# A written order for three engines through the third chunk's heads, narrower expert widths, an early drain

## The chip, the cores and the metric

The kernel runs on one core of a Trainium2 chip. The metric is device time in microseconds (us) of one execution; lower is better. Engines: PE (TensorE), DVE (VectorE), ACT (ScalarE), POOL (GpSimd) and SP (SyncE, which only starts transfers). Each takes its instructions from its own queue, in order, and waits for the others at semaphores.

## The reference

Three layers stand behind one another, all in float32:

```python
scores = scale * np.matmul(q, k.transpose(0, 1, 3, 2))     # 4 batches, 8 heads, 576 positions, 64 wide
scores = np.where(mask, scores + bias[None], -1000000000.0) # mask: 0 <= i - j < 128
attn = np.exp(scores - scores.max(-1)) ; attn = attn / (attn.sum(-1) + 1e-9)
x = attn @ v                                                # as (2304 tokens, 512)
x = (sigmoid(x @ w_gate) * (x @ w_val)) @ w_out             # 512 -> 1536 -> 512
expert_idx = argmax(normalised x @ normalised expert_emb.T / tau)
for e in range(8):
    mask = expert_idx == e
    h = np.maximum(x[mask] @ w1[e], 0.0)                    # 512 -> 1024
    out[mask] = gate_w[mask, None] * (h @ w2[e])            # 1024 -> 512
```

## The kernel before

The 2304 tokens are 18 blocks of 128, in chunks of 2, 2, 2, 4, 4 and 4 blocks. A product in float32 is made of three matmuls: each operand is split into a high part, rounded to the matmul's format, and a low part, the rest; high x high, high x low and low x high are summed. So each operand costs a copy (the high part) and a subtraction (the low part) on ACT, DVE or POOL.

**Attention.** The first two chunks are done in pairs of heads (`fast_s`, `fast_n`, `fast_t`, `fast_b`): scores on PE, a reduction with the bias on DVE, exponentials on ACT, the scaling of the rows by one over their sum (`scale_rows`: "v" is DVE, "p" is POOL, by the table `NE`; its two entries are for the two chunks), a transpose on PE, a copy by ACT into `ttf`, and the product with v. From the third chunk on each head is a slot `i`: `load_qkv`, `split_qkv`, `load_v`, `split_v`, `emit_s`, `emit_soft`, `emit_norm`, `emit_t` (transposes, and the parts `ph` on ACT and `pl` on DVE), `emit_pv` (the product with v) and `emit_x` (the head's output).

**Work between the heads.** The weights w_gate and w_val come as 64-bit words. `feed_w(n)` takes n conversion steps: `conv_b` (three DVE operations), and for every second step the split of a weight tile (`split_hi` on ACT writes `wh`, `split_lo` on DVE writes `wl`). `run_group` is one tile of the gated layer: `group_mm` (24 matmuls) and `group_post`. `GR` says how many groups follow each head, `FS` and `FW` how many conversion steps.

**What sets the order.** Inside `manual_schedule` the order of PE, DVE and ACT is that in which the code is written: this holds for the head pairs. POOL's and SP's queues, and everything behind that block, are ordered by a scheduler. `tc.issue_after(ins)` keeps what is written under it behind the instruction `ins` (in the scheduler's order). Before, the third chunk's first loads and splits are held behind the last instruction of four engines in pair `SLOW` (`marks`) and behind the last load of the second chunk.

**Experts.** The tokens are sorted by expert with indirect transfers on POOL. Experts are taken in order of their size as far as `CAPS` knows it: `CAPS[e]` is the number of columns that the e-th has in `ffn1` (the tiles `h`) and of rows in `ffn2` (the tiles `z`, one for 128 tokens, then scaled to `y` and scattered by an indirect transfer to `out`). If an expert has more tokens than its capacity, a loop at the end does the rest. The program ends with a closing block (line 1203) in which each engine executes DRAIN instructions.

Of the kernel before, what the change touches and what calls it, by code (L numbers as in the profile page):

```python
# [1 line left out]

# [1 line left out]

# [21 lines left out]
E = 8  # L26
# [4 lines left out]
KD = DM // P  # L31
KF = FF // P
KE = FE // P
CAPS = [384, 384, 384, 352, 320, 320, 288, 256]
TCOL = NBLK
MAXOV = 16
BIG = 2.0 ** 42
# [6 lines left out]
NFAST = 2  # L44
NWARM = 12
FW = [[0, 0], [0, 1], [0, 1], [0, 1], [1, 1], [1, 1], [0, 1], [0, 1]]
FG = [0, 0, 0, 0, 0, 0, 1, 1]
FS = [3] + [2] * 7 + [0] * 24
FIRST = [0, 1] * 6
SLOW = 5  # L50
NE = ["vpvp", "vpvp"]
NR = "aapp"
GR = [3, 2, 3, 2, 3, 2, 3, 2, 2] + [2, 1, 1, 2, 1, 2, 1, 2] + [2] * 15
CHUNKS = [2, 2, 2, 4, 4, 4]
# [4 lines left out]
def attn_ffn_moe(ctx: ExitStack, tc: tile.TileContext, qd, kd, vd, wgv, w_out, emb, tau, w1, w2, cst, ids, out):  # L59
# [36 lines left out]
    def hi_copy(eng, o, i):  # L96
        if eng == "a":
            nc.scalar.copy(o, i)  # L98
        elif eng == "v":
            nc.vector.tensor_copy(o, i)  # L100
        else:
            nc.gpsimd.tensor_scalar(out=o, in0=i, scalar1=1.0, scalar2=0.0, op0=ALU.mult, op1=ALU.add)
# [67 lines left out]
    def split_qkv(i):  # L170
        c, h = slots[i]
        b0, nb = chunks[c]
        n = nb * P
        lo = 0 if b0 else 1
        q_t, k_t = raw.pop(i)[:2]
        qs = ap.tile([P, 512], F32R, tag="qs", name=f"qs{i}")
        k1 = ap.tile([P, 640], F32R, tag="k1", name=f"k1{i}")
        k2 = ap.tile([P, 640], F32R, tag="k2", name=f"k2{i}")
        hi_copy("p" if c == NFAST else QE, qs[:, :n], q_t[:, :n])
        lo_sub("p", qs[64:128, :n], q_t[64:128, :n], qs[64:128, :n])  # L180
        ks = slice(lo * P, n + P)
        hi_copy("p" if c == NFAST else KE_, k1[:, ks], k_t[:, ks])
        lo_sub("v", k2[:, ks], k_t[:, ks], k1[:, ks])
        bias = bias_of(h)
        bsp = {}
        for j in range(nb):
            kind = {4: 1, 13: 1, 5: 2, 14: 2}.get(b0 + j)
            if kind:
                t = row(f"bsp{i}_{j}")[:, 0:256]
                hi_copy("p", t, bias)  # L190
                nc.gpsimd.memset(t[64:128, 0:192] if kind == 1 else t[:, 0:64], -BIG)
                bsp[j] = t
        spl[i] = (qs, k1, k2, bias, bsp)
# [152 lines left out]
    def load_fast(c, lo, hi):  # L346
        b0 = chunks[c][0]
        ts = slice(b0 * P, b0 * P + 256)
        if lo == 0:
            for dst, nm in ((fq, "fq"), (fk, "fk")):  # L350
                dst[c] = slot([P, 4, 256], F32, f"{nm}{c}")
        for dst, src in ((fq, qd), (fk, kd)):
            pairs = src.rearrange("(g u) d t -> u d g t", u=2)
            for u in range(2):
                half = slice(u * D, u * D + D)
                nc.sync.dma_start(dst[c][half, lo:hi, :], pairs[u, half, lo:hi, ts])

    def load_fast_v(c):
        b0 = chunks[c][0]
        t = slot([P, H, 2, D], F32, f"fv{c}")  # L360
        fv[c] = t
        return nc.sync.dma_start(t, vd[:, :, b0:b0 + 2, :].rearrange("h p b d -> p h b d"))
# [63 lines left out]
    def fast_b(c, g):  # L426
        b0, nb = chunks[c]
        n = nb * P
        nm = f"f{c}_{g}"
        tts, fks = fst.pop((c, g))  # L430
        o = pt("m", f"o{nm}", 3)
        kbs = list(range(-1 if fks[0] == 0 else 0, nb))
        for z, kb in enumerate(kbs):
            q0, q1 = max(kb, 0), min(kb + 2, nb)
            c0 = (2 * kb + 1 + (q0 - kb)) * P
            for u in range(2):
                nc.tensor.matmul(o[u * D:u * D + D, q0 * P:q1 * P], fv[(b0 + kb) // 2][:, 2 * g + u, (b0 + kb) % 2, :],
                                 tts[u][:, c0:c0 + (q1 - q0) * P], start=(z == 0), stop=(z == len(kbs) - 1),
                                 skip_group_check=True)
        xh, xl = split_x_hi(c, 2 * g + 1, n, o)  # L440
        return lambda: lo_sub("v", xl, o[:, :n], xh)
# [20 lines left out]
    def split_hi(f):  # L462
        wh, wl = slot([P, 2, KD, P], F32R, f"wh{f}"), slot([P, 2, KD, P], F32R, f"wl{f}")
        hi_copy("a", wh, w_a[f])
        w_t[f] = (wh, wl)

    def split_lo(f):
        wh, wl = w_t[f]
        lo_sub("v", wl, w_a.pop(f), wh)
# [53 lines left out]

    NS = len(slots)
    NW = 2 * KF
    wnext = [0, 0]

    def feed_load(n):
        while wnext[0] < min(NW, n):
            load_w(wnext[0])  # L530
            wnext[0] += 1

    def feed_w(n):
        for _ in range(n):
            j = wnext[1]
            if j > NW:
                return
            feed_load(j + 8)
            if j == 0:
                conv_a(0)  # L540
            if j < NW:
                conv_b(j)
            if j % 2 == 0 and j:
                split_lo(j // 2 - 1)
            if j + 1 < NW:
                conv_a(j + 1)
            if j % 2 == 1:
                split_hi(j // 2)
            wnext[1] += 1

    def run_group(c, fs, gv):
        group_post(c, fs, gv, group_mm(c, fs, gv))
# [3 lines left out]
    load_fast(0, 1, 2)  # L556
    load_fast(0, 2, 4)
    load_fast_v(0)
    feed_load(3)
    load_fast(1, 0, 4)  # L560
    last_load = load_fast_v(1)
    warm = cp.tile([P, 512], BF16, tag="warm", name="warm")
    nc.vector.memset(warm, 0.0)
# [8 lines left out]
    with tc.manual_schedule(engines={ENG.PE, ENG.DVE, ENG.Activation}):  # L572
        for _ in range(NWARM):
            nc.tensor.matmul(wp, warm[:, 0:P], warm, start=True, stop=True)
        pairs = [(c, g) for c in range(NFAST) for g in range(H // 2)]
        fast_s(*pairs[0])
        fast_s(*pairs[1])
        fast_n(*pairs[0])
        late, post = [], []
        for i, (c, g) in enumerate(pairs):  # L580
            fast_t(c, g)
            if i + 1 < len(pairs):
                fast_n(*pairs[i + 1])
            for t in late:
                t()
            feed_w(FW[i][0])
            if i + 2 < len(pairs):
                fast_s(*pairs[i + 2])
            late = [fast_b(c, g)]
            feed_w(FW[i][1])  # L590
            if i == H // 2 - 1:
                push_first()
            for gr, m in post:
                group_post(*gr, m)
            post = []
            for _ in range(FG[i]):
                gr = queue.pop(0)
                post.append((gr, group_mm(*gr)))
            if i == SLOW:
                marks = latest(ENG.PE, ENG.DVE, ENG.Activation, ENG.Pool)  # L600
        for t in late:
            t()
        for gr, m in post:
            group_post(*gr, m)
    with ExitStack() as behind:
        for ins in marks + [last_load.ins]:
            behind.enter_context(tc.issue_after(ins))
        load_qkv(0)
        load_v(0)
        nc.sync.dma_start(ids_sb, ids)  # L610
        split_qkv(0)
        load_qkv(1)
        split_v(0)
        load_v(1)
        split_qkv(1)
        load_qkv(2)
        emit_s(0)
        emit_soft(0)
        emit_norm(0)
    for i in range(NS):  # L620
        c, h = slots[i]
        if i > 0:
            emit_x(i - 1)
        if h == 1 and c > NFAST:
            push_groups(c - 1)
        if i + 1 < NS:
            emit_s(i + 1)
            emit_soft(i + 1)
        if i + 2 < NS:
            split_qkv(i + 2)  # L630
        if i + 3 < NS:
            load_qkv(i + 3)
        if i + 1 < NS:
            split_v(i + 1)
        if i + 2 < NS:
            load_v(i + 2)
        feed_w(FS[i])
        todo = []
        while queue and len(todo) < GR[i]:
            todo.append(queue.pop(0))  # L640
        done = []
        if todo:
            done.append((todo[0], group_mm(*todo[0])))
        emit_t(i)
        if i + 1 < NS:
            emit_norm(i + 1)
        for g, m in done:
            group_post(*g, m)
        for g in todo[1:]:
            run_group(*g)  # L650
        emit_pv(i)
# [437 lines left out]
    hs = ffn1_tok(0, CE)  # L1089
    ffn2(0, CE, 0, hs, col(0, CE))  # L1090
    for e in range(1, E):
        if e + 1 < E:
            for t in tiles(e + 1):
                gather(e + 1, t, col(e + 1, t), w=width(e + 1, t))
            weights(e + 1)
        t0 = EARLY[e] if e < len(EARLY) else 0
        hs = ffn1(e, CAPS[e] - t0 * P)
        if e + 1 < E:
            make_x(e + 1, CAPS[e + 1])
        for t in tiles(e):  # L1100
            if e + 1 < E and t in tiles(e + 1):
                transp(e + 1, t, t, width(e + 1, t))
            if t >= t0:
                ffn2(e, t, t - t0, hs, col(e, t), width(e, t))

    pn, pe, pb, po = small("pn", E), small("pe", E), small("pb", E), small("po", E)
    pi, cu = small("pi", E, I32), small("cu", E)
# [99 lines left out]
```

## Time and profile before

| what | us |
|---|---|
| median of three timed runs (918.13 to 920.56) | 918.26 |
| the profiled execution | 916.44 |
| its span, first to last instruction | 914.4 |
| PE busy in the span | 874.6 |
| DVE busy | 546.6 |
| ACT busy | 437.9 |
| POOL busy | 240.3 |

The profiled execution is 2.04 us longer than its span. Rows come from one execution. A line `A <- B` in the waits names what the engine waited for; a duration in a timeline is that of the instructions in the row, and the bracket holds the engine's idle time ahead of them and what ended it. PE's matmuls overlap, so the distance between two starts, not the duration of one, is what a matmul costs.

### The profile page before, as it was taken

The numbers are of one execution on the slowest core, as the hardware profiler recorded it, in microseconds if no ns is written. First come the engines' busy times: TensorE is split into PE (matmuls) and PEld (weight loads), VectorE is DVE, ScalarE is ACT, GpSimd is POOL, SyncE is SP. The second block draws the span as 40 slices with busy tenths as digits, with TensorE's granted clock in tenths as the row PEclk, the third lists the DMA queues.
The fourth block names the chain that finished last, engine by engine and source line by source line (L and its number), as shares of the span: only waits on it lengthen the run. The fifth ranks groups of instructions, "written<-read, shape, count | busy, mean of one in ns | idle before, by whom it ended". The sixth has DMA issues, their size and how long they took to land. (4 is left out here: it accounts for less than half of the span.)

```text
span 914.4 us, 14453 instructions
## 1 busy us (share of the span) xinstructions
PE 874.6 (96%) x5080; PEld 750.2 (82%) x5080; DVE 546.6 (60%) x1352; ACT 437.9 (48%) x943; POOL 240.3 (26%) x305
## 2 busy tenths in 40 slices
PE   6888999899999999999999999999999999999995
PEld 3578989899888888888878888888878989888874
DVE  4988967878888755564205554443855545445442
ACT  5666746676666663342215554443534334333330
POOL 2265624455655530000000000022130221230220
PEclk9788999999999999999999999999999999999998
DMA  7745434334333222483114345514356544553500
GB/s 205 267 145 184 148 106 127 101 117 131 109 122 128 90 96 84 150 273 115 47 47 116 116 139 137 160 50 128 98 169 206 198 158 157 173 191 126 170 25 15
DMA packets 69738, 121.69 MB, mean 133 GB/s; under 512 B 8280, under 2 KB 37080, under 8 KB 69666
## 3 DMA queue, kind: packets, MB, share of 16 engines
q1 hardware_dynamic: 65666, 110.53, 38.1%
q0 software_dynamic: 4000, 10.25, 3.4%
q8 instruction: 40, 0.66, 0.3%
q14 instruction: 32, 0.26, 0.1%
HBM read 97.06 MB, written 24.47 MB: 133 GB/s over the span
## 5 line engine op out<-in xcount | busy, mean ns | idle before, releaser
L482 PE MATMUL m<-x,wh 128*128 128x256 f32 (+1 forms) x1152 | 289.5, 342 | 0.0
L482 PEld LDWEIGHTS m<-x,wh 128*128 128x128 f32 x1152 | 198.2, 193 | 21.1 <-issue 0.5
L482 PE MATMUL m<-x,wl 128*128 128x256 f32 (+1 forms) x576 | 195.4, 339 | 0.0
L794 PE MATMUL y<-wo,gh 128*128 128x512 f32 x432 | 141.3, 401 | 0.0
L482 PEld LDWEIGHTS m<-x,wl 128*128 128x128 f32 x576 | 110.6, 192 | 11.4
L967 PE MATMUL h<-xe,weh 128*128 128x256 f32 (+4 forms) x512 | 107.6, 302 | 1.3 <-DVE lg L829 1.0
L983 PE MATMUL z<-weh,h 128*128 128x512 f32 (+3 forms) x336 | 106.6, 396 | 0.0
L794 PEld LDWEIGHTS y<-wo,gh 128*128 128x128 f32 x432 | 80.0, 188 | 17.4
L114 DVE TENSOR_TENSOR wel<-wer,weh 128x1024 fp32r<-128x1024 f32 x64 | 78.2, 1222 | 18.5 <-ACT weh L98 16.5
L967 PEld LDWEIGHTS h<-xe,weh 128*128 128x128 f32 x512 | 84.6, 188 | 4.1 <-DVE h L970 1.3
L794 PE MATMUL y<-wo,gl 128*128 128x512 f32 x216 | 86.0, 398 | 0.0
L967 PE MATMUL h<-xe,wel 128*128 128x256 f32 (+4 forms) x256 | 77.1, 301 | 0.0
L969 ACT ACTIVATE h<-h 128x256 fp32r<-128x256 f32 (+4 forms) x64 | 27.2, 425 | 95.6 <-PE h L967 94.4
L988 POOL DMA_INDIRECT out<-y,cols x20 | 26.5, 1324 | 172.6 <-DVE y L987 159.1
L983 PEld LDWEIGHTS z<-weh,h 128*128 128x128 f32 (+3 forms) x336 | 58.3, 178 | 15.2
L98 ACT CAST weh<-wer 128x1024 fp32r<-128x1024 f32 x64 | 66.1, 1044 | 6.1 <-DMA wer<-in_w 6.0
L881 POOL DMA_INDIRECT tab_d<-ids_sb,ai x18 | 18.3, 1016 | 186.4 <-DVE ai L878 169.8
L983 PE MATMUL z<-wel,h 128*128 128x512 f32 (+3 forms) x168 | 65.8, 392 | 0.0
L496 DVE SCALAR_TENSOR_TENSOR sg<-sg,m 128x512 f32<-128x512 f32 x54 | 36.8, 681 | 47.1 <-PE m L482 32.8
L250 ACT ACTIVATE p<-p,mx 128x256 f32<-128x256 f32 x112 | 55.3, 494 | 13.5 <-DVE mx L247 12.5
L492 ACT ACTIVATE sg<-m 128x512 f32<-128x512 f32 x54 | 32.1, 594 | 61.0 <-PE m L482 60.3
L810 ACT ACTIVATE xr<-y 128x512 f32<-128x512 f32 x18 | 10.8, 598 | 93.5 <-PE y L794 93.5
(212 smaller groups left out, 1555.1 us busy)
## 6 DMA issues: line engine op xcount, KB each, us to landing
wer<-in_w SPq DMA_DIRECT2D x64, 512.0 KB, 4.7
gT_d<-sg SPq DMA_DIRECT2D x54, 256.0 KB, 2.4
gl<-gT_d SPq DMA_DIRECT2D x27, 512.0 KB, 6.2
wr<-in_wgv SPq DMA_DIRECT2D x24, 512.0 KB, 6.1
kr<-in_kd SPq DMA_DIRECT2D x24, 320.0 KB, 3.1
qr<-in_qd SPq DMA_DIRECT2D x24, 256.0 KB, 2.7
wor<-in_w_out SPq DMA_DIRECT2D x12, 512.0 KB, 4.0
x_d<-xr SPq DMA_DIRECT2D x18, 256.5 KB, 4.7
```

Of the source, the lines that this page charges most:

```text
L98: nc.scalar.copy(o, i)
L114: e.tensor_tensor(out=o, in0=i, in1=h.bitcast(F32), op=ALU.subtract)
L250: nc.scalar.activation(out=p_t[:, j, f:], in_=p_t[:, j, f:], func=AF.Exp, scale=-1.0, bias=mx[:, j:j + 1], accum_out=su[:, j:j + 1])
L482: nc.tensor.matmul(m[:, z * n:(z + 1) * n], w[:, gv, k, :], x[k], start=(cnt == 0), stop=(cnt == 3 * KD - 1))
L492: nc.scalar.activation(out=sg[:, 0:512], in_=m, func=AF.Tanh, scale=0.5)
L496: nc.vector.scalar_tensor_tensor(out=sg[:, 0:512], in0=sg[:, 0:512], scalar=1.0, in1=m, op0=ALU.add, op1=ALU.mult)
L794: nc.tensor.matmul(m, g[:, k % 4, u * P:(u + 1) * P], w[:, k % 3, :], start=(k == 0 and z == 0), stop=(k == KF - 1 and z == 2))
L881: nc.gpsimd.indirect_dma_start(out=tab_d, out_offset=IOA(ap=ai[:, u:u + 1], axis=0), in_=ids_sb[:, t:t + 1], in_offset=None)
L967: nc.tensor.matmul(m[:, :n], w[:, fs], x[:, k, :], start=(cnt == 0), stop=(cnt == 3 * KD - 1))
L969: nc.scalar.activation(out=hh, in_=m[:, :n], func=AF.Relu)
L983: nc.tensor.matmul(m[0:w, :], h, ww[:, ds], start=(cnt == 0), stop=(cnt == 3 * KE - 1))
L988: nc.gpsimd.indirect_dma_start(out=out, out_offset=IOA(ap=idx[0:w], axis=0), in_=y[0:w, :], in_offset=None, bounds_check=NT - 1, oob_is_er ...
```

## The change

`CAPS` gives the sixth expert (rank 5) 288 and the seventh (rank 6) 256 columns in place of 320 and 288. POOL gets a drain in its queue ahead of the last expert, and the last expert's second product is put behind PE's latest instruction. In the attention stage the third chunk's eight heads go into the block with the written order; each head's groups stand between its transposes and `emit_pv`, and a conversion step may follow each group. The split that writes a weight's high part (`split_hi`) is kept back by a list and done by `flush_hi()` behind the next exponentials. Nothing but the last load of the second chunk holds the third chunk's first loads, and nothing holds `split_qkv(0)`. `NE` gives the second chunk's scalings all to POOL, and the third chunk's high part of k goes from POOL to ACT ("a"). One weight load stands ahead of the second chunk's loads in place of three, and one between its k and its v. The `hi_copy` and `scale_rows` calls only change engine.

POOL's queue before, from the last bias on (`pf0_0` and `pf0_1` are the scores of the first chunk's first two pairs, `rsf` their factors):

```order
L152 TENSOR_SCALAR bias4_202<-cs_75 128x256 x4
L110 TENSOR_SCALAR pf0_0_134<-pf0_0_134,rsf0_0_167 128x256 [waits DVE_49,Activation_49]
L110 TENSOR_SCALAR pf0_0_134<-pf0_0_134,rsf0_0_167 128x256 [waits Activation_49]
L110 TENSOR_SCALAR pf0_1_154<-pf0_1_154,rsf0_1_186 128x256 [waits DVE_49,Activation_49]
L110 TENSOR_SCALAR pf0_1_154<-pf0_1_154,rsf0_1_186 128x256 [waits Activation_49]
```

POOL's queue now, from the same place on (`qs0`, `qs1` are the split q of the third chunk's first two heads, `qr0`, `qr1` their loads, `bsp` biases with a masked part):

```order
L152 TENSOR_SCALAR bias4_200<-cs_75 128x256 x4
L102 TENSOR_SCALAR bsp0_0_537<-bias0_135 128x256 [waits Pool_49]
L102 TENSOR_SCALAR bsp0_1_540<-bias0_135 128x256
L191 MEMSET bsp0_0_537 64x192 [waits Pool_49]
L191 MEMSET bsp0_1_540 128x64 [waits Pool_49]
L102 TENSOR_SCALAR bsp1_0_621<-bias0_135 128x256
L102 TENSOR_SCALAR bsp1_1_624<-bias0_135 128x256
L191 MEMSET bsp1_0_621 64x192 [waits Pool_49]
L191 MEMSET bsp1_1_624 128x64 [waits Pool_49]
L102 TENSOR_SCALAR qs0_530<-qr0_389 128x256 [waits DMAHW5_49]
L114 TENSOR_TENSOR qs0_530<-qr0_389,qs0_530 64x256 [waits Pool_49]
L110 TENSOR_SCALAR pf0_0_132<-pf0_0_132,rsf0_0_165 128x256 [waits DVE_49,Activation_49,Pool_49]
```

Ten instructions have moved ahead of the first scaling of `pf0_0`; the ninth waits for a transfer (before, the split of `qr0` stood behind the scaling of the second chunk's third pair). On ACT, around the second chunk's last pairs, before (`wh1`, `wh2` are high parts of weights, `pf1_2` and `pf1_3` exponentials of the third and fourth pair):

```order
L118 ACTIVATE wa2_416<-wr4_268 128x512
L98 CAST wh1_418<-wa1_332 128x1024
L397 ACTIVATE pf1_2_429,suf1_2_431<-pf1_2_429,mxf1_2_430 128x256 x4
L98 CAST x0_1_0_447<-of1_0_440 128x256
L118 ACTIVATE wa2_416<-wr5_270 128x512
L422 COPY ttf1_1_0_462<-tf1_1_0_457 128x512
L422 COPY ttf1_1_1_469<-tf1_1_1_464 128x512
L118 ACTIVATE wa3_484<-wr6_272 128x512
L98 CAST wh2_486<-wa2_416 128x1024
L397 ACTIVATE pf1_3_497,suf1_3_499<-pf1_3_497,mxf1_3_498 128x256 x4
```

And now, at the same place of ACT's queue:

```order
L118 ACTIVATE wa2_423<-wr4_268 128x512
L397 ACTIVATE pf1_2_433,suf1_2_435<-pf1_2_433,mxf1_2_434 128x256 x4
L98 CAST wh1_444<-wa1_332 128x1024
L98 CAST x0_1_0_454<-of1_0_447 128x256
L118 ACTIVATE wa2_423<-wr5_270 128x512
L422 COPY ttf1_1_0_469<-tf1_1_0_464 128x512
L422 COPY ttf1_1_1_476<-tf1_1_1_471 128x512
L118 ACTIVATE wa3_491<-wr6_272 128x512
L397 ACTIVATE pf1_3_501,suf1_3_503<-pf1_3_501,mxf1_3_502 128x256 x4
L98 CAST wh2_512<-wa2_423 128x1024
```

The copies `wh1` and `wh2` have changed places with the exponentials of `pf1_2` and `pf1_3`.

```diff
--- before.py
+++ after.py
@@ -1,4 +1,4 @@
-from contextlib import ExitStack
+from contextlib import ExitStack, nullcontext
 
 import numpy as np
 
@@ -31,7 +31,7 @@
 KD = DM // P
 KF = FF // P
 KE = FE // P
-CAPS = [384, 384, 384, 352, 320, 320, 288, 256]
+CAPS = [384, 384, 384, 352, 320, 288, 256, 256]
 TCOL = NBLK
 MAXOV = 16
 BIG = 2.0 ** 42
@@ -45,10 +45,10 @@
 NWARM = 12
 FW = [[0, 0], [0, 1], [0, 1], [0, 1], [1, 1], [1, 1], [0, 1], [0, 1]]
 FG = [0, 0, 0, 0, 0, 0, 1, 1]
-FS = [3] + [2] * 7 + [0] * 24
+FS = [2, 2, 1, 1, 2, 1, 1, 0]
 FIRST = [0, 1] * 6
 SLOW = 5
-NE = ["vpvp", "vpvp"]
+NE = ["vpvp", "pppp"]
 NR = "aapp"
 GR = [3, 2, 3, 2, 3, 2, 3, 2, 2] + [2, 1, 1, 2, 1, 2, 1, 2] + [2] * 15
 CHUNKS = [2, 2, 2, 4, 4, 4]
@@ -179,7 +179,7 @@
         hi_copy("p" if c == NFAST else QE, qs[:, :n], q_t[:, :n])
         lo_sub("p", qs[64:128, :n], q_t[64:128, :n], qs[64:128, :n])
         ks = slice(lo * P, n + P)
-        hi_copy("p" if c == NFAST else KE_, k1[:, ks], k_t[:, ks])
+        hi_copy("a" if c == NFAST else KE_, k1[:, ks], k_t[:, ks])
         lo_sub("v", k2[:, ks], k_t[:, ks], k1[:, ks])
         bias = bias_of(h)
         bsp = {}
@@ -523,7 +523,7 @@
 
     NS = len(slots)
     NW = 2 * KF
-    wnext = [0, 0]
+    wnext, pend = [0, 0], []
 
     def feed_load(n):
         while wnext[0] < min(NW, n):
@@ -541,12 +541,17 @@
             if j < NW:
                 conv_b(j)
             if j % 2 == 0 and j:
+                flush_hi()
                 split_lo(j // 2 - 1)
             if j + 1 < NW:
                 conv_a(j + 1)
             if j % 2 == 1:
-                split_hi(j // 2)
+                pend.append(j // 2)
             wnext[1] += 1
+
+    def flush_hi():
+        while pend:
+            split_hi(pend.pop(0))
 
     def run_group(c, fs, gv):
         group_post(c, fs, gv, group_mm(c, fs, gv))
@@ -556,8 +561,9 @@
     load_fast(0, 1, 2)
     load_fast(0, 2, 4)
     load_fast_v(0)
-    feed_load(3)
+    feed_load(1)
     load_fast(1, 0, 4)
+    feed_load(2)
     last_load = load_fast_v(1)
     warm = cp.tile([P, 512], BF16, tag="warm", name="warm")
     nc.vector.memset(warm, 0.0)
@@ -586,6 +592,10 @@
             feed_w(FW[i][0])
             if i + 2 < len(pairs):
                 fast_s(*pairs[i + 2])
+            elif i + 1 == len(pairs):
+                emit_s(0)
+                emit_soft(0)
+            flush_hi()
             late = [fast_b(c, g)]
             feed_w(FW[i][1])
             if i == H // 2 - 1:
@@ -596,28 +606,49 @@
             for _ in range(FG[i]):
                 gr = queue.pop(0)
                 post.append((gr, group_mm(*gr)))
+            if i == SLOW - 2:
+                with tc.issue_after(last_load.ins):
+                    load_qkv(0)
+                    load_v(0)
+                    nc.sync.dma_start(ids_sb, ids)
             if i == SLOW:
-                marks = latest(ENG.PE, ENG.DVE, ENG.Activation, ENG.Pool)
+                split_qkv(0)
+                load_qkv(1)
+                flush_hi()
+            if i == SLOW + 1:
+                split_v(0)
+                load_v(1)
+                split_qkv(1)
+                load_qkv(2)
         for t in late:
             t()
-        for gr, m in post:
-            group_post(*gr, m)
-    with ExitStack() as behind:
-        for ins in marks + [last_load.ins]:
-            behind.enter_context(tc.issue_after(ins))
-        load_qkv(0)
-        load_v(0)
-        nc.sync.dma_start(ids_sb, ids)
-        split_qkv(0)
-        load_qkv(1)
-        split_v(0)
-        load_v(1)
-        split_qkv(1)
-        load_qkv(2)
-        emit_s(0)
-        emit_soft(0)
         emit_norm(0)
-    for i in range(NS):
+        for i in range(H):
+            c, h = slots[i]
+            if i > 0:
+                emit_x(i - 1)
+            emit_s(i + 1)
+            emit_soft(i + 1)
+            emit_t(i)
+            for gr, m in post:
+                group_post(*gr, m)
+            post = []
+            flush_hi()
+            todo = [queue.pop(0) for _ in range(GR[i])]
+            for z, gr in enumerate(todo):
+                post.append((gr, group_mm(*gr)))
+                if z == 0:
+                    split_qkv(i + 2)
+                    load_qkv(i + 3)
+                    split_v(i + 1)
+                    load_v(i + 2)
+                    emit_norm(i + 1)
+                feed_w(FS[i] if z == 0 else 1 - z // 2)
+                if z + 1 < len(todo):
+                    gr, m = post.pop(0)
+                    group_post(*gr, m)
+            emit_pv(i)
+    for i in range(H, NS):
         c, h = slots[i]
         if i > 0:
             emit_x(i - 1)
@@ -634,7 +665,9 @@
             split_v(i + 1)
         if i + 2 < NS:
             load_v(i + 2)
-        feed_w(FS[i])
+        for gr, m in post:
+            group_post(*gr, m)
+        post = []
         todo = []
         while queue and len(todo) < GR[i]:
             todo.append(queue.pop(0))
@@ -1089,6 +1122,8 @@
     hs = ffn1_tok(0, CE)
     ffn2(0, CE, 0, hs, col(0, CE))
     for e in range(1, E):
+        if e + 1 == E:
+            tc.keep_in_program_order(nc.gpsimd.drain())
         if e + 1 < E:
             for t in tiles(e + 1):
                 gather(e + 1, t, col(e + 1, t), w=width(e + 1, t))
@@ -1101,7 +1136,8 @@
             if e + 1 < E and t in tiles(e + 1):
                 transp(e + 1, t, t, width(e + 1, t))
             if t >= t0:
-                ffn2(e, t, t - t0, hs, col(e, t), width(e, t))
+                with tc.issue_after(latest(ENG.PE)[0]) if e + 1 == E else nullcontext():
+                    ffn2(e, t, t - t0, hs, col(e, t), width(e, t))
 
     pn, pe, pb, po = small("pn", E), small("pe", E), small("pb", E), small("po", E)
     pi, cu = small("pi", E, I32), small("cu", E)
```

## Rows read from the trace of the kernel before

**Rows 1.** The page's first part: busy us, share, instructions.

```profile
PE 874.6 (96%) x5080; PEld 750.2 (82%) x5080; DVE 546.6 (60%) x1352; ACT 437.9 (48%) x943; POOL 240.3 (26%) x305
```

**Rows 2.** Windows of 20 us in the attention stage.

```profile
core 0: us, PE busy (x) PEld busy (x) DVE busy (x) ACT busy (x) POOL busy (x), PEclk, DMA share, GB/s
0.00:20.00 20.00, 14.75 (x78) 7.82 (x78) 9.04 (x52) 10.70 (x39) 6.41 (x19) 0.91 0.73 203
20.00:40.00 20.00, 14.72 (x92) 9.98 (x94) 17.12 (x54) 13.21 (x37) 2.99 (x6) 0.80 1.02 328
...
80.00:100.00 20.00, 16.74 (x119) 16.35 (x118) 18.45 (x40) 12.25 (x25) 9.89 (x18) 0.83 0.51 159
100.00:120.00 20.00, 20.00 (x171) 20.00 (x170) 18.66 (x37) 13.46 (x29) 11.76 (x15) 1.00 0.28 86
```

**Rows 3.** PE's waits from 0 to 320 us: total, times, longest.

```profile
PE o L307 <- DVE pl L114: 5.5, 7, 1.8
PE of L437 <- ACT ttf L422: 5.1, 4, 3.2
PE o L307 <- ACT ph L98: 3.5, 2, 2.6
```

**Rows 4.** PE's timeline in the experts of rank 5, 6 and 7.

```profile
819.31 0.31 PE L967 MATMUL h<-xe,wel 128*128 128x320 f32 x1
...
821.07 0.31 PE L967 MATMUL h<-xe,wel 128*128 128x320 f32 x1
...
844.66 0.43 PE L947 MATMUL tx<-cs,xg 32*128 32x32 f32 x4
845.02 0.67 PE L983 MATMUL z<-weh,h 128*64 128x512 f32 x2
...
850.56 0.43 PE L967 MATMUL h<-xe,weh 128*128 128x288 f32 x2
...
856.51 0.43 PE L967 MATMUL h<-xe,weh 128*128 128x288 f32 x2
...
885.74 0.39 PE L967 MATMUL h<-xe,weh 128*128 128x256 f32 x2
...
886.76 0.39 PE L967 MATMUL h<-xe,weh 128*128 128x256 f32 x2
```

**Rows 5.** The page's groups: low parts of the experts' weights.

```profile
L114 DVE TENSOR_TENSOR wel<-wer,weh 128x1024 fp32r<-128x1024 f32 x64 | 78.2, 1222 | 18.5 <-ACT weh L98 16.5
```

**Rows 6.** The closing block's DRAINs on POOL: ns min/median/max, first to last start.

```profile
L1203 POOLq DRAIN  x3: 46/103/5302, 907.9 to 913.8; - x3
```

**Rows 7.** POOL's timeline in the first 32 us.

```profile
6.50 3.34 POOL L152 TENSOR_SCALAR bias<-cs 128x256 f32<-128x256 f32 x8 [5.55 <-DMA cs<-in_cst]
10.74 0.95 POOL L110 TENSOR_SCALAR pf<-pf,rsf 128x256 f32<-128x256 f32 x2 [0.90 <-DVE rsf L405]
```

**Rows 8.** The load `qr` in the first 30 us: its issue and landing.

```profile
L166 SPq DMA_DIRECT2D qr<-in_qd x1: 3607/3607/3607, 15.8 to 15.8; - x1
...
DMA to landing us min/median/max: 10.2/10.2/10.2
```

**Rows 9.** POOL's timeline where it splits `qr0`.

```profile
43.73 0.61 POOL L102 TENSOR_SCALAR qs<-qr 128x256 fp32r<-128x256 f32 x1
...
45.34 1.05 POOL L114 TENSOR_TENSOR qs<-qr,qs 64x256 fp32r<-64x256 f32 x1
```

**Rows 10.** PE's timeline: the first matmul of the gated layer.

```profile
52.58 0.80 PE L482 MATMUL m<-x,wh 128*128 128x256 f32 x2
```

**Rows 11.** DVE's timeline from 20 to 30 us.

```profile
20.84 0.43 DVE L124 TENSOR_SCALAR wa<-wa 128x512 int32<-128x512 int32 x1 [1.84 <-ACT wa L118]
21.30 0.69 DVE L125 SCALAR_TENSOR_TENSOR wa<-wr,wa 128x512 int32<-128x512 int32 x1
...
25.61 0.42 DVE L394 CUSTOM_DVE_ANT_0 pf<-sf,bias 128x256 f32<-128x256 f32 x1 [1.52 <-PE sf L384]
...
29.19 0.84 DVE L108 TENSOR_SCALAR pf<-pf,rsf 128x256 f32<-128x256 f32 x2
```

## The prediction

> **What bounds the kernel now.** I read the page's first part, then the windows of the attention stage, then PE's waits, and only then single rows. The first part says that PE is busy in 874.6 of 914.4 us [rows 1]: whatever takes matmuls away counts in full, and whatever only moves other engines counts where PE idles. The profiled execution took 916.44 us, 2.04 us more than its span; the median of the three timed runs is 918.26 us, 1.8 us above it. The sum below is made against 916.44, and the forecast is set about 1 us above the sum for that difference.
>
> The windows show where PE idles, in the first 60 us, and what is the limit there: DVE is busy in 17.12 of the 20 us from 20 on, in 18.45 from 80 on and in 18.66 from 100 on [rows 2]. So the front of the program is DVE's, with PE behind it, and from 100 us on PE is full. PE's granted clock, 0.80 in the second window and 0.83 from 80 to 100, is below 1.0 behind such waits. The waits name them: PE's product with the attention weights waits 5.5 us in 7 times for the low part `pl` from DVE and 3.5 us in 2 times for `ph` from ACT; in the fast heads `of` waits 5.1 us for ACT's `ttf` [rows 3].
>
> **Widths.** In the default inputs (worked out from the reference) the experts in order of rank have 346, 358, 339, 323, 280, 270, 222 and 166 tokens. They fit the old and the new capacities, so the overflow loop stays empty in both. What the narrower widths take off PE:
> - Rank 5, h 320 to 288 columns: from 819.31 to 821.07 lie twelve matmuls of 320 columns, 0.1467 us each; from 850.56 to 856.51 forty-five of 288, 0.1322 us each [rows 4]. An expert has 96 of them (8 tiles of h, 4 pieces of the 512 inputs, 3 matmuls each): 96 x 0.0145 = 1.4 us.
> - Rank 6, 288 to 256: from 885.74 to 886.76 nine of 256 columns, 0.1133 us each [rows 4]. 96 x 0.0189 = 1.8 us.
> - Rank 6 loses its third tile of 32 tokens. Its second product is priced by rank 5's third tile, the same 24 matmuls of 512 columns: from 845.02 to 850.56, 5.54 us; ahead of them four transposes, from 844.66 to 845.02, 0.36 us [rows 4]. Rank 5's own third tile goes from 64 to 32 rows of tokens and keeps its 512 columns: nothing.
> - Together 9.1 us. Work that stood under rank 6's third tile moves up to expert 7: on DVE the low parts of its weights, 1.22 us each [rows 5], now come close behind the last scaling of rank 6. I take 0.5 us of wait for it, between 0 and 1.2. Net **-8.6 us** (-9.1 to -7.9).
>
> The order put on the last expert's second product (`issue_after` on PE's latest) only puts its first tile wholly behind the eight h tiles; the matmuls are the same and the weights have been there: 0. If its cover failed, one weight split would show, 1.2 us [rows 5].
>
> **The drain.** Behind the last scatter, the closing block holds a DRAIN on POOL of 5.302 us from 907.9 on, and POOL's two others there take 0.05 and 0.10 us [rows 6]. Nothing else runs. The change puts a drain into POOL's queue before the last expert, where POOL has nothing to do until that expert's scatters, and PE's work covers it. Two bounds. If the 5.3 us pays for what the indirect transfers of the whole program have left behind, the early drain pays for nearly all, and the last one keeps what two scatters leave: **-4.9 us**. If it is a price of the last drain as such, 0. The two short ones beside it say that a drain with nothing left behind costs 0.1 us, which is nearer to the first; I take -4.9. The Trainium skill ("VectorE: DVE Perf Modes", The DRAIN you can't avoid) tells of drains in the pre- and postamble as a constant of about 12 ns. By that there would be nothing to move and the sum would be 4.9 us higher; the 5302 ns row speaks against a constant of that size, and no row shows what it depends on.
>
> **The front.** This is where the change can lose. `split_qkv(0)` was held behind marks of four engines; now nothing holds it, and the order of POOL shows where it comes: two instructions on `qs0` stand ahead of the first scaling of `pf0_0`. POOL's queue is in order, and the first of them waits for the load `qr0`. Before, POOL scales `pf0_0` at 10.74 us [rows 7], long before that load: it is issued at 15.8 and lands 10.2 us later, at 26.0 [rows 8]. In the new load order one weight load of 512 KB less stands ahead of it; at the 328 GB/s of that window [rows 2] this is 1.6 us, so 24.4. Then POOL makes `qs0` (0.61) and its low part (1.05) [rows 9] and scales `pf0_0` at about 26.1 instead of 10.74: **+15.3 us**. Behind POOL stand PE (its `tf` matmuls need the scaled rows, and the next pair's `sf` are queued behind them), and behind PE in turn DVE and ACT. SP's `qr1`, `qr2` and the weight loads from `wr2` on also wait for POOL's splits; they have been issued early enough before not to be the next thing late.
>
> What comes back by the first matmul of the weight stage, which starts at 52.58 [rows 10]: DVE's wait of 1.52 for `sf`, which waited for the second chunk's loads [rows 11], since all of them land during the stall: -1.5. `NE` gives the second chunk's four pairs wholly to POOL: 4 x 0.84 us off DVE [rows 11], -3.4. The high parts of the weights, which wait on ACT for DVE, now stand behind the exponentials; of the 5.1 us that `of` waits for `ttf` [rows 3] I take 2 as gained, between 0 and 5.1: -2.0. Then the first slot's softmax is put in ahead, about 1.4 us of DVE by two reductions like those of 0.42 [rows 11] and a low part of k (estimate). Sum 15.3 - 1.5 - 3.4 - 2.0 + 1.4 = **+9.8 us**. Bounds: +15.3 if nothing comes back, +6 if the waits for `ttf` go too.
>
> **The third chunk.** The written order puts the groups between the transposes and `pv`, so that `pl` and `ph` have some 6 us of PE work to come in. It can win at most the 9.0 us of these waits [rows 3] and some clock; but DVE has only 1.6 and 1.3 us free of 20 in the windows there [rows 2], so PE can't run ahead of it. The high part of k moves from POOL to ACT: neither is the limit. Head 1 gets one conversion step more, 0.43 + 0.69 + 0.69 = 1.8 us of DVE [rows 11]. I take **-4 us**, between -9 and +2.
>
> **Sum.** 916.44 - 8.6 - 4.9 + 9.8 - 4 = 908.7; with 1 us for the median **910 us**.
>
> **Rivals.**
> - *The drain does not move* (a price of the closing drain as such). For it: nothing in the trace shows what it depends on. Against: the short ones beside it. 908.7 + 4.9 + 1 = 915 us, at the edge of no change.
> - *The stall is not there or is taken back whole* (the load lands far earlier, since little else is ahead of it then, or the third chunk had slack for it). For: PE idles about a quarter of the first 60 us [rows 2], so part of a stall may fall on idle time. Against: DVE is nearly full from 20 to 120 us, so its lost time has no place to be made up. 916.44 - 8.6 - 4.9 + 1 = 904 and down to 899 with the third chunk's gain.
> - *Slower: DVE carries the stall through the third chunk.* DVE's lost 15.3 us stay whole, and in the written order each head's `pv` on PE is stuck behind DVE's posts and conversion steps, where before PE could take groups meanwhile. It decides where front and third chunk together cost more than 16.3 us, that is 13.5 of gains and the 2.75 us of the bound. By its price, +15.3 for the front and +2 to +5 for the first heads (one conversion step in each of them on PE's path), 916.44 - 13.5 + 15.3 + 3.5 + 1 = 923 us. For: the saturated DVE [rows 2]. Against: the recovered waits have rows.
> - *The change of order changes nothing*, since the engines follow the same data: then widths and drain alone, the 904 us above.
>
> **How the numbers follow.** About 0.3%, 2.75 us, can be told from no change by a measurement of this kernel. Forecast (stall, partly recovered, drain moves: 905 to 914) 0.42; drain fixed (911 to 918) 0.20; no stall or a full recovery (898 to 905) 0.15; slower by DVE's front (918 to 926) 0.23. Faster, below 915.5: nearly all of the first, half of the second, all of the third: 0.66. Slower, above 921.0: 0.17 of the last case and a little of the second: 0.19. Same: 0.15. The range leaves out 1 in 10 on either side: 900 to 922; the forecast's own is 905 to 914.
>
> **What will show it.** In the profile after: POOL's first `pf` scaling at about 26 us with a wait for `qr` ahead of it (right), or near 11 (wrong); the first `m` matmul at about 62 us; PE's waits for `pl` and `ph` below 3 us; no third tile in the seventh expert, and the h matmuls of 288 and 256 columns; a DRAIN on POOL near 880 us of some 5 us and a short one at the end. Wrong it would be if the closing DRAIN still takes 5 us, or if `m` starts as before, or if PE loses more than 10 us between 60 and 320 us.

## The result and the profile after

The changed kernel is slower: 928.92 us in the median of five runs (926.19 to 929.24) against 918.26 us (917.63 to 920.81) for the kernel before, a ratio of 1.0101 with the interval 1.0079 to 1.0123. The span of the profiled execution went from 914.4 to 926.4 us. The page's first part of the changed kernel answers to [rows 1]: PE has 6.9 us less to do and takes 12 us longer over it.

```profile
PE 867.7 (94%) x5052; PEld 743.0 (80%) x5052; DVE 544.2 (59%) x1342; ACT 439.2 (47%) x950; POOL 227.8 (25%) x303
```

To find the 12 us I set marks in both traces and took differences: the start of the first `m` matmul; that of the 721st `m` matmul (behind 30 groups of 24, which lie in the fast heads' end, the third chunk and the beginning of the fourth); the first matmul of an expert's second product `z`; the end of the last one; the end of the span.

| stretch | before | after | difference |
|---|---|---|---|
| start to first `m` | 52.6 | 64.5 | +11.9 |
| first to 721st `m` | 134.2 | 143.2 | +9.0 |
| 721st `m` to first `z` | 460.4 | 462.0 | +1.6 |
| first `z` to end of the last | 256.1 | 250.6 | -5.4 |
| last `z` to the end of the span | 11.1 | 6.0 | -5.1 |

The +1.6 in the third row is no effect of the change: five kernels whose code is that of the kernel before up to the experts (e2, e3, e10, e11, e12, below) take 461.8 to 462.8 us there.

**The front.** POOL's timeline of the changed kernel (start, duration; idle time ahead and what ended it in brackets) answers to [rows 7] and [rows 9]:

```profile
11.82 0.49 POOL L191 MEMSET bsp<- 64x192 f32 x2
23.85 0.40 POOL L102 TENSOR_SCALAR qs<-qr 128x256 fp32r<-128x256 f32 x1 [11.54 <-DMA qr<-in_qd]
24.34 0.72 POOL L114 TENSOR_TENSOR qs<-qr,qs 64x256 fp32r<-64x256 f32 x1
25.16 1.84 POOL L110 TENSOR_SCALAR pf<-pf,rsf 128x256 f32<-128x256 f32 x4
```

POOL stands idle for 11.54 us until `qr` has landed, and scales `pf0_0` at 25.16 us, where it did at 10.74. PE's timeline shows the other end of the same wait, and where the gated layer then starts, which answers to [rows 10] (`of` is the product with v in the fast heads, `tf` the transpose ahead of it):

```profile
25.69 1.33 PE L420 MATMUL tf<-cs,pf 128*128 128x128 f32 x5 [13.84 <-POOL pf L110]
...
62.11 2.45 PE L437 MATMUL of<-ttf,fv 128*64 128x128 f32 x12 [3.35 <-ACT ttf L422]
64.49 0.80 PE L482 MATMUL m<-x,wh 128*128 128x256 f32 x2
```

**The third chunk.** PE's longest waits over the whole span (total, times, longest) answer to [rows 3]:

```profile
PE tf L420 <- POOL pf L110: 14.3, 2, 13.8
PE of L437 <- ACT ttf L422: 9.5, 5, 3.3
PE o L307 <- DVE pl L114: 5.2, 6, 1.6
PE m L482 <- ACT sg L492: 4.1, 3, 2.8
PE m L482 <- DVE sg L496: 3.3, 2, 1.9
PE tf L420 <- DVE pf L108: 2.4, 2, 2.0
PE o L307 <- ACT ph L98: 2.2, 1, 2.2
```

The waits for `pl` and `ph` were to go; they are 7.4 us where they were 9.0, and the groups' matmuls themselves now wait 7.4 us for `sg`, the post of an earlier group that must free its PSUM tile; the kernel before has no such wait. DVE's waits from 62 to 212 us say who is late in turn:

```profile
DVE pl L114 <- ACT ph L98: 14.7, 12, 1.8
DVE p L247 <- PE s L231: 4.7, 3, 3.2
DVE k L114 <- ACT k L98: 4.0, 4, 1.5
```

In the kernel before, in the same stretch (52 to 190 us), the first of these waits is

```profile
DVE pl L114 <- ACT ph L98: 4.5, 6, 1.5
```

Between the first head's output `xf` and the eighth's, that is in seven heads, it is 0.9 us in one wait before (76 to 145 us), and in the changed kernel (86 to 163 us) one wait for each head:

```profile
DVE pl L114 <- ACT ph L98: 9.9, 7, 1.8
```

One such wait, in the timelines of DVE and of ACT at the same head:

```profile
102.25 0.42 DVE L247 CUSTOM_DVE_ANT_0 p<-s,bsp 128x256 f32<-128x256 f32 x1
...
103.96 0.69 DVE L114 TENSOR_TENSOR pl<-t,ph 128x512 fp32r<-128x512 f32 x1 [1.28 <-ACT ph L98]
...
102.37 0.51 ACT L250 ACTIVATE p<-p,mx 128x256 f32<-128x256 f32 x1
...
102.88 0.49 ACT L250 ACTIVATE p<-p,mx 128x256 f32<-128x256 f32 x1
...
103.37 0.56 ACT L98 CAST ph<-t 128x512 fp32r<-128x512 f32 x1
```

In the written order ACT makes the two exponentials of head i+1 before `ph` of head i, and DVE has `pl` of head i directly behind the two reductions that these exponentials wait for. So DVE stands still for two exponentials and a copy in each head, with conversion steps waiting behind it.

**The end.** The DRAINs of POOL's closing block, which answer to [rows 6], and the early one (durations in ns):

```profile
L1239 POOLq DRAIN  x3: 46/103/215, 925.2 to 926.1; - x3
...
L1126 POOLq DRAIN  x1: 6939/6939/6939, 896.6 to 896.6; - x1
```

The 5.302 us have become 0.215, and 6.939 us lie beside the last expert's matmuls.

### The profile page after: what moved, and what is told of

It is laid out like the page before. It is cut to its first block, busy times and chain, and to the rows that moved or that the text cites. A ratio compares the mean times of both kernels' runs of the same rounds, so it can differ in the third digit from the quotient of the medians.

```text
span 926.4 us, 14378 instructions
## 1 busy us (share of the span) xinstructions
PE 867.7 (94%) x5052; PEld 743.0 (80%) x5052; DVE 544.2 (59%) x1342; ACT 439.2 (47%) x950; POOL 227.8 (25%) x303
## 5 line engine op out<-in xcount | busy, mean ns | idle before, releaser
L1016 PE MATMUL z<-weh,h 128*128 128x512 f32 (+3 forms) x320 | 101.8, 396 | 0.0
L1016 PEld LDWEIGHTS z<-weh,h 128*128 128x128 f32 (+3 forms) x320 | 56.4, 180 | 14.0
L1016 PE MATMUL z<-wel,h 128*128 128x512 f32 (+3 forms) x160 | 62.8, 393 | 0.0
```

The lines of the kernel that those rows point to most:

```text
L1016: nc.tensor.matmul(m[0:w, :], h, ww[:, ds], start=(cnt == 0), stop=(cnt == 3 * KE - 1))
```

## Experiments

The times of one group of runs were taken on one chip beside runs of the kernel before; ratios are to that kernel, with a 95% interval. The marks come from one profiled execution each. Between six kernels with the attention stage of before (before, e2, e3, e10, e11, e12) the way from the first to the 721st `m` is 133.8 to 137.7 us, so differences of under 4 us in it say nothing. The first `m` starts at 52.0 to 53.2 us in these six, and at 49.9 to 50.9 in the four with the changed front and the hold of e1 (e1, e5, e6, e7).

| kernel | median us | ratio | first `m` | first to 721st `m` |
|---|---|---|---|---|
| changed | 928.92 | 1.0101 [1.0079, 1.0123] | 64.5 | 143.2 |
| e1 splits held on POOL | 913.7 | 0.9932 [0.9910, 0.9953] | 49.9 | 140.9 |
| e4 scheduler in third chunk | 914.75 | 0.9949 [0.9932, 0.9966] | 65.3 | 128.8 |
| e5 both | 905.57 | 0.9838 [0.9810, 0.9865] | 50.9 | 136.1 |
| e6 e1 and a step ahead of t | 908.95 | 0.9879 [0.9851, 0.9908] | 50.4 | 137.3 |
| e7 e1 and posts first | 913.79 | 0.9939 [0.9920, 0.9959] | 50.6 | 142.9 |
| e8 e1 and k on POOL | 913.06 | 0.9923 [0.9899, 0.9947] | 51.6 | 142.9 |
| e9 e5 with shared scalings | 903.88 | 0.9853 [0.9806, 0.9899] | 52.5 | 130.4 |
| e2 before, widths alone | 914.94 | 0.9945 [0.9925, 0.9964] | 53.2 | 137.7 |
| e3 before, drain alone | 915.09 | 0.9942 [0.9920, 0.9963] | 52.9 | 136.7 |
| e10 before, widths and drain | 910.96 | 0.9925 [0.9897, 0.9954] | 52.3 | 133.9 |
| e12 e10 a second time | 910.69 | 0.9914 [0.9895, 0.9933] | 52.0 | 133.8 |
| e11 e10 and the tile order | 907.09 | 0.9866 [0.9845, 0.9888] | 52.9 | 134.1 |

**e1, the first splits held on POOL.**

```diff
             if i == SLOW:
-                split_qkv(0)
+                with tc.issue_after(latest(ENG.Pool)[0]):
+                    split_qkv(0)
                 load_qkv(1)
...
             if i == SLOW + 1:
-                split_v(0)
-                load_v(1)
-                split_qkv(1)
+                with tc.issue_after(latest(ENG.Pool)[0]):
+                    split_v(0)
+                    load_v(1)
+                    split_qkv(1)
```

> The changed kernel with the third chunk's first two splits held on POOL behind its latest instruction, so that POOL scales pf0_0 first again. Theory A (the stall of 15 us is POOL waiting for qr0, and the third chunk loses its 9 us by the written order itself): the first m matmul moves from 64.5 to about 49 us, and the time from 928.9 to about 913 us, with the way from the first to the 720th m matmul as long as now (143 us). Theory B (the third chunk loses only because the stall has put DVE behind): the stall goes and most of the 9 us too, about 904 to 906 us, and that way takes 134 us as before.

Theory A held for the front. POOL scales `pf0_0` at 11.33 us again and the first `m` starts at 49.89:

```profile
11.33 0.95 POOL L110 TENSOR_SCALAR pf<-pf,rsf 128x256 f32<-128x256 f32 x2 [1.68 <-DVE rsf L405]
...
49.89 0.80 PE L482 MATMUL m<-x,wh 128*128 128x256 f32 x2
```

The time falls by 0.0169 of the kernel before, 15.5 us: the whole stall. The way behind it stays long, 140.9 us, and DVE's waits for `ph` are the same 14.9 us in 12 times. From the first head's `xf` to the eighth's the changed kernel takes 76.0 us and e1 75.9. So the third chunk's loss is not a consequence of the stall.

**e4, the scheduler orders the third chunk.** The loop over its eight heads stands outside the block with the written order, and `emit_norm(0)` ahead of it too; nothing else differs.

```diff
     with tc.manual_schedule(engines={ENG.PE, ENG.DVE, ENG.Activation}):
...
         for t in late:
             t()
-        emit_norm(0)
-        for i in range(H):
-            c, h = slots[i]
+    emit_norm(0)
+    for i in range(H):
+        c, h = slots[i]
```

> The changed kernel with the third chunk's heads taken out of the block of the written order, so that the scheduler orders PE, DVE and ACT there; the POOL stall stays. Theory A (the written order costs the 9 us): 919 to 921 us, with the first m matmul still near 64 us. Theory B (the stall's backlog costs them): 927 to 930 us, no difference.

It gained more than theory A gave: 14 us. The stall is there (first `m` at 65.3), but the way to the 721st `m` is 128.8 us, shorter than any way of the kernel before. DVE is busy in 34.05 of 40 us from 60 us on, where in the changed kernel it is in 30.05:

```profile
60.00:100.00 40.00, 37.04 (x296) 35.29 (x297) 34.05 (x77) 30.01 (x69) 18.54 (x33) 0.92 0.52 167
100.00:140.00 40.00, 36.20 (x294) 34.91 (x294) 37.03 (x76) 26.06 (x58) 17.63 (x20) 1.00 0.34 107
```

and in the changed kernel (columns as in [rows 2]):

```profile
60.00:100.00 40.00, 35.85 (x276) 33.70 (x277) 30.05 (x62) 23.98 (x53) 13.20 (x23) 0.91 0.50 151
100.00:140.00 40.00, 33.87 (x259) 32.43 (x259) 32.44 (x68) 24.92 (x57) 13.56 (x26) 0.96 0.29 87
```

**e5, both mends.** The edits of e1 and of e4 together.

> Both mends at once: the first splits held on POOL, and the third chunk's heads ordered by the scheduler. If the two losses add up (15 us for the stall, 14 us for the written order), about 928.9 - 29 = 900 us, the first m matmul near 50 us and the way from the first to the 720th m matmul 129 us. If the short way of 129 us came only from work that was done ahead during the stall, that way is 134 to 138 us as in the kernel before, and the time 905 to 909 us.

The losses don't add: 905.57 us, and a way of 136.1 us, as in the kernels with the old attention stage. With the scheduler the hold is worth 0.0111 (10 us), with the written order 0.0169 (15.5 us). So a part of the stall, 5 us known to about 4, can be made up behind it, and the written order doesn't make it up. Where the scheduler makes it up is not shown: the short way of e4 need not come from work done during the stall, since e9, which has no stall and differs from e5 in one table, has a way of 130.4 us.

**e6, a conversion step ahead of the transposes.** On top of e1; the number of steps in a head stays.

```diff
             emit_soft(i + 1)
+            feed_w(min(FS[i], 1))
             emit_t(i)
...
-                feed_w(FS[i] if z == 0 else 1 - z // 2)
+                feed_w(max(FS[i] - 1, 0) if z == 0 else 1 - z // 2)
```

> The changed kernel with the first splits held on POOL, and in each of the third chunk's heads one conversion step moved ahead of the transposes, so that DVE has work while ACT makes ph. If DVE's waits for ph (14.7 us in 12 times) are what makes the written order slow, 913.7 - 5 to 10 = 904 to 909 us. If DVE's own work or PE's wait for the posts sets the pace, 912 to 916 us.

This names a part of the loss inside the written order: 0.9879 against 0.9932, 4.9 us (3.3 us either way), in the expected range. DVE's waits from 48 to 200 us, in e1 and then in e6:

```profile
DVE pl L114 <- ACT ph L98: 14.9, 12, 1.8
```

```profile
DVE pl L114 <- ACT ph L98: 5.2, 6, 1.8
```

The waits fall by 9.7 us and the time by half of that. From the third head's `xf` to the fourth's DVE takes 9.5 us in e6 (95.05 to 104.56) and 10.2 in e1 (96.20 to 106.45), and from the first to the eighth 71.7 in place of 75.9. PE's waits for `sg` (0 to 320 us) fall with them, from 6.1 us in e1 to 1.9.

**e7, posts ahead of the steps; e8, k back on POOL.** Both on top of e1.

```diff
-                feed_w(FS[i] if z == 0 else 1 - z // 2)
                 if z + 1 < len(todo):
                     gr, m = post.pop(0)
                     group_post(*gr, m)
+                feed_w(FS[i] if z == 0 else 1 - z // 2)
```

> The changed kernel with the first splits held on POOL, and in the third chunk's heads each group's post ahead of the conversion steps in place of behind them. If PE's waits for the posts (sg, 6 to 7 us in 5 times) are the loss, 907 to 909 us and no m matmul waits for sg. If PE then waits for pl or wl instead, 912 to 915 us.

```diff
-        hi_copy("a" if c == NFAST else KE_, k1[:, ks], k_t[:, ks])
+        hi_copy("p" if c == NFAST else KE_, k1[:, ks], k_t[:, ks])
```

> The changed kernel with the first splits held on POOL, and the third chunk's high part of k back on POOL. If ACT's load makes ph late (0.5 us for k stand in ACT's queue in each head), 910 to 912 us. If not, no difference, 913 to 915 us; POOL's slower copies could add to DVE's wait for k, then 915 to 917 us.

Neither differs from e1 (0.9939 and 0.9923 against 0.9932). In e7 the matmuls still wait 6.6 us for `sg`: so the posts' place behind a step is not what makes them late; that they are late because DVE as a whole is fits e6, but no run shows it by itself. In e8 DVE's waits for `ph` stay at 15.5 us.

**e9, the second chunk's scalings shared again.** On top of e5.

```diff
-NE = ["vpvp", "pppp"]
+NE = ["vpvp", "vpvp"]
```

> The kernel with both mends (splits held on POOL, third chunk ordered by the scheduler), with the second chunk's scalings shared by DVE and POOL again. The prediction put 3.4 us of DVE's work on this table. If DVE sets the pace of the front, the first m matmul goes from 50.9 to 53 or 54 us and the time from 905.6 to 908 or 909. If POOL's four scalings in a row cost the pair as much as DVE saves, no difference, 904 to 907 us.

The first `m` comes 1.6 us later than in e5 (1.6 to 2.6 later than in the four kernels with that front), half to three quarters of what DVE's work would give, in one trace; the time does not tell the two apart (0.9853 and 0.9838, with overlapping intervals).

**e2, e3 and e10, the expert stage in the kernel before.** e2 has only the new `CAPS`, e3 only the early drain, e10 both.

```diff
-CAPS = [384, 384, 384, 352, 320, 320, 288, 256]
+CAPS = [384, 384, 384, 352, 320, 288, 256, 256]
```

```diff
     for e in range(1, E):
+        if e + 1 == E:
+            tc.keep_in_program_order(nc.gpsimd.drain())
```

> The kernel before with the new CAPS alone. The sum of the prediction gives -8.6 us: 909.7 us. In the changed kernel the last expert's h tiles take 13.6 us where 96 matmuls of 256 columns should take 10.9. If the narrower seventh expert causes that (its followers come too early for DVE's low parts), the gain is about 6 us: 912 us. If the tile order on the last expert causes it, it is 8.6.

> The kernel before with the early drain alone. By the trace of the changed kernel (closing DRAIN 0.215 us, the early one 6.9 us beside PE's work) -5.1 us: 913.2 us. If the early drain holds something up behind it on POOL (the last expert's scatters), less: 916 us or more.

> The kernel before with the new widths and the early drain and nothing else. If the two are independent, 918.3 x 0.9945 x 0.9942 = 908 us. The part of the change that orders the attention stage is worth what the kernel with both mends (0.9838 of before, 903.4 by the same reckoning) is below that: 4 to 5 us if the terms hold, none if this run comes to 904.

The widths alone are worth 5.1 us (1.8 us either way), the drain 5.3 (2.0 either way) by the medians' ratios; both together 6.9 (e10) and, a second time, 7.9 (e12), where their sum would be 10.4. By the traces the drain shortens the way from the last `z` to the end of the span from 11.1 to 6.2 us (e3), and the widths that from the first `z` to the last from 256.1 to 251.0 us (e2). Of the 9.1 us of matmuls that the widths take away, some 2 go at the start of rank 6 and 7, in waits of PE's timeline of e2:

```profile
829.26 0.41 PE L947 MATMUL tx<-cs,xg 128*128 128x128 f32 x2 [1.26 <-DMA xg<-x_d,cols]
...
882.44 0.50 PE L967 MATMUL h<-xe,wel 128*128 128x256 f32 x2 [0.17 <-DVE wel L114]
883.76 0.50 PE L967 MATMUL h<-xe,weh 128*128 128x256 f32 x2 [0.82 <-DVE h L970]
```

The traces also show where the rest went. From one expert's first `h` matmul to the next one's, rank 5 takes 31.7 us where it took 32.0, and rank 6 23.5 where it took 30.3: 7.1 us less, not 9.1. The last expert, whose 144 matmuls are the same, takes 24.2 us from its first `h` to its last `z` matmul where it took 22.0 (22.4 in e3). In it PE's weight loads wait for DVE, in e2 (860 to 900 us) and then in the kernel before (850 to 912 us):

```profile
PEld h L967 <- DVE h L970: 1.7, 4, 1.0
PEld h L967 <- DVE wel L114: 0.7, 2, 0.4
```

```profile
PEld h L967 <- DVE h L970: 0.4, 1, 0.4
```

e2 has no tile order, so it is the widths that make the last expert slow: behind a shorter rank 6, DVE's parts of the last expert come too late.

And e2's way from the last `z` to the end has grown from 11.1 to 12.7 us, and e10's is 8.0, where the drain alone has 6.2. POOL's timeline of e10 shows why:

```profile
898.60 0.99 POOL L988 DMA_INDIRECT out<-y,cols  x1 [21.17 <-DVE y L987]
902.11 0.98 POOL L988 DMA_INDIRECT out<-y,cols  x1 [2.52 <-DMA out<-y,cols]
```

The last expert's two tiles end close together there, and the second scatter waits 2.52 us for the first one to land. In the kernel before the two scatters start 5.0 us apart (899.28 and 904.32) with no such wait; the new widths bring them together. The tile order parts them again, so the next run has it too.

**e11 and e12, the tile order.** e12 repeats e10 on the chip of e11.

```diff
             if t >= t0:
-                ffn2(e, t, t - t0, hs, col(e, t), width(e, t))
+                with tc.issue_after(latest(ENG.PE)[0]) if e + 1 == E else nullcontext():
+                    ffn2(e, t, t - t0, hs, col(e, t), width(e, t))
```

> The kernel before with the new widths, the early drain and the tile order on the last expert. The prediction gave the tile order 0. The trace of the kernel with widths and drain shows the last two scatters 3.5 us apart, the second waiting 2.5 us for the first to land; with the tile order they would be 5.5 us apart with no such wait. If that is right, the way from the last z to the end of the span goes from 8.0 to 6.1 us, and the time is 2 us below the kernel without the tile order. If the time is set elsewhere, no difference.

> The kernel before with the new widths and the early drain alone, a second time, on the same chip as the kernel with the tile order too: 907 to 911 us, and 2 us above it if the tile order parts the last two scatters.

It is so: the ratio goes from 0.9914 to 0.9866, and the way from the last `z` to the end from 8.0 to 6.0 us. The scatters of e11 stand 5.5 us apart, and the wait for the landing is gone:

```profile
894.07 0.99 POOL L988 DMA_INDIRECT out<-y,cols  x1 [17.18 <-DVE y L987]
899.57 0.98 POOL L988 DMA_INDIRECT out<-y,cols  x1 [4.50 <-DVEq L1145]
```

The trace explains 2 us of the 4.4 between the two ratios; their intervals allow 0.6 to 8. With e11 (0.9866) beside e5 (0.9838) it is open whether the new attention stage, with both mends, is worth anything: the intervals overlap. The 721st `m` starts at 187.0 us in the traces of both, and at 182.9 in e9.

## Why the prediction was wrong

- **The step that failed is the third chunk**: "I take -4 us, between -9 and +2". It was +9.0, so 13 of the 19 us between the sum (908.7) and the profiled execution (928.16) lie here. The argument looked at PE's queue alone, on which `pl` and `ph` get more cover, and took DVE's idle time as a bound on the gain. It didn't ask what DVE and ACT wait for when their own order is fixed too. The runs show it: each head makes DVE wait for two exponentials and `ph`, 14.7 us in all where it was 4.5 before (e6 takes 9.7 us of these waits away and gets 4.9 us of time back; the posts' place and k make no difference in e7 and e8). Against the scheduler's order the written one costs 0.0094 (8.6 us) without the stall (e1 and e5) and 14 with it (changed kernel and e4). Against e11, which has the same expert stage and the attention stage of before, e1 is 0.0066 (6 us) slower though its first `m` comes 3 us earlier. What costs the rest beside `ph`, some 4 us without the stall (e6 and e5), is open.
- **The front: the mechanism was right, the sum a little small** (+9.8 forecast, +11.9 measured). The stall was forecast at 15.3 us and is 14.4 (25.16 against 10.74). Of the 5.5 us that were to come back in all 2.5 did. The table `NE` gave about 2 us, not 3.4 (e9), and the waits for `ttf` rose from 5.1 to 9.5 us where 2 were to go: with the high parts behind the exponentials they were not shorter. No run moves the high parts alone.
- **The drain was right**: -5.1 us in the trace, 5.3 in e3, -4.9 forecast. The Trainium skill ("VectorE: DVE Perf Modes", The DRAIN you can't avoid) tells of a constant of about 12 ns. For POOL it does not hold here: [rows 6] show 5.302 us, the changed kernel 0.215 at the same place. The DRAINs of the other engines in the same block of the kernel before take 7 to 17 ns, near that constant.
- **The widths were oversized**: -8.6 forecast; the expert stage became 5.4 us shorter in the changed kernel, and 5.1 in e2. PE's 9.1 us of work are gone, but rank 6's gathered rows now come too late (0.98 us in the changed kernel, 1.26 in e2, no wait in e11), and so do DVE's low parts in the last expert. In the changed kernel the last expert takes 24.3 us from its first `h` to its last `z` matmul, 2.3 more than before; the prediction allowed 0.5 for that and nothing for the rows. The remaining 0.7 us went within rank 6.
- **The tile order was put at 0 and is worth about 2 us beside the new widths**: the prediction looked at PE alone, on which nothing changes, and not at the two scatters behind it, which the widths bring so close that the second waits for the first.
- **The slower rival** had the right sign (923 us) and half the cause. DVE did carry the stall into the third chunk, and by e4 and e5 beside the changed kernel and e1 the written order keeps some 5 us of it that the scheduler gives back. The other half, what the written order costs without any stall, it did not have. Its place was wrong too: `pv` doesn't wait longer than before (7.4 against 9.0 us), the groups do (7.4 against none).

## What to carry to other kernels

When a hold is taken away in a program whose order is made by a scheduler, list the queue of each engine: one instruction that waits for a transfer, ahead of an early one on an engine with little to do, cost the whole program 15 us. A written order must be laid out for all engines at once: put independent work between a producer on one engine and its consumer on the next, as the conversion step in e6. And a price at the end of a program can be paid early where another engine covers it; what the last two transfers wait for belongs to that end.

## What had not been expected of the hardware

The closing DRAIN on POOL takes 5.302 us in the kernel before and 5.138 in e2, and 0.215 to 0.220 us wherever another one ended some 20 us earlier. The early one is dearer than the one that it replaces (6.94 and 7.00 us in two kernels).

POOL's scaling of four pieces took 1.84 us while DVE had nothing to do (25.16), and 2.94 us in the second chunk's later pairs. A busy DVE alone does not explain that: at 42.29 the four took 1.84 us too, with DVE busy all the time, mostly with reductions (L394). They are slow where they lie beside a conversion step's instructions with two operands (L125, L127), and these are slow there as well: 0.77 and 0.85 us against 0.69 without POOL. In the changed kernel:

```profile
42.29 1.84 POOL L110 TENSOR_SCALAR pf<-pf,rsf 128x256 f32<-128x256 f32 x4 [3.60 <-ACT ttf L422]
47.54 2.94 POOL L110 TENSOR_SCALAR pf<-pf,rsf 128x256 f32<-128x256 f32 x4 [3.40 <-DVE rsf L405]
...
42.33 0.41 DVE L394 CUSTOM_DVE_ANT_0 pf<-sf,bias 128x256 f32<-128x256 f32 x1
...
45.17 0.69 DVE L127 SCALAR_TENSOR_TENSOR wa<-wr,wa 128x512 int32<-128x512 int32 x1
...
48.03 0.77 DVE L125 SCALAR_TENSOR_TENSOR wa<-wr,wa 128x512 int32<-128x512 int32 x1
48.83 0.85 DVE L127 SCALAR_TENSOR_TENSOR wa<-wr,wa 128x512 int32<-128x512 int32 x1
```

Whether this is why the table `NE` gave less than the work that it took off DVE, no run shows.
